# Attention with 16 queries against 2048 keys: another layout and place for the query load, two heads per matmul in P·V, and another order of work at the end

## The chip, the cores and the metric

The kernel runs on one core of one Trainium2 chip. The metric is device time in microseconds (us), taken as the median of several executions; lower is better. A core has a matrix engine (PE, with weight loads listed apart as PEld), a vector engine (DVE), a scalar engine (ACT), a general engine (POOL) and a sync engine (SP), which here issues all data transfers. Sixteen DMA engines move the data (the page gives the DMA shares as parts of 16). All executions quoted here are in the undisturbed ("fast") state.

## The reference

```python
B, H, Sq, Skv, Dh = 8, 16, 16, 2048, 256          # q, k, v in bf16
def reference(q, k, v):
    scale = q.shape[-1] ** -0.5
    scores = jnp.einsum('bhqd,bhkd->bhqk', q, k) * scale
    attn = softmax(scores, axis=-1)
    return jnp.einsum('bhqk,bhkd->bhqd', attn, v)
```

There are 128 heads (B·H). Each has only 16 queries, but its K and its V are 1 MB each. So 256 tiles of 1 MB are read, plus 1 MB of Q, and 1 MB of output is written.

## The kernel before

Four heads make a "quad"; there are 32 quads, numbered 0 to 31. For each head K is transposed on PE (16 f32 transposes, two bf16 values packed in each, into three buffers `stg` in PSUM, the memory in which this program puts PE's results; DVE and ACT copy them to `ktb`). For each quad come the scores (32 matmuls into `s_ps`, the four heads in four 32-column strips of the array), the max on DVE, the exp on ACT, the transposes of P (8), and P·V, called PV below (64 matmuls into `o_ps`). The order of work on PE is fixed in this list:

```python
NK = 4; NV = 8; NKT = 6; NSTG = 3       # K slots, V slots, transposed K, staging banks
# ... all Q transposes come first ...
for n in range(NQ):                      # NQ = 32 quads
    TK(4 * n)                            # transpose K of a head
    if n > 0: TP(n - 1)                  # transpose P of the quad before
    TK(4 * n + 1)
    if n > 0: pe_tasks.append(("PV", n - 1))
    TK(4 * n + 2)
    TK(4 * n + 3)
    pe_tasks.append(("S", n))            # scores
TP(NQ - 1)
pe_tasks.append(("PV", NQ - 1))
```

SP issues the loads in a fixed order too. A load waits until its slot is free, and then joins a queue of loads that are already on the way (five to eight of them for 246 of the 257 loads in the trace of the kernel before):

```python
sp.dma_start(qraw[:], qf).then_inc(sem_q, 16)     # Q first, in rows of 256 elements
# ... K and V alternate, V two heads behind K ...
for h in range(6, NH - 2):
    sp_loads.append(("K", h)); sp_loads.append(("V", h - VLAG))
sp_loads += [("K", NH - 2), ("K", NH - 1)] + [("V", h) for h in range(NH - 4, NH)]
```

And PV, one head per matmul, four heads side by side in four strips:

```python
for t in range(KT_T):                    # 16 pieces of 128 keys
    b, et = divmod(t, 2)
    for j in range(4):
        h = 4 * n + j
        c0 = (b * 128 + 32 * j) * 2
        lhs = ptb[:, n % 2, c0:c0 + 32].rearrange("p (q e) -> p q e", e=2)[:, :, et]
        last = pe.matmul(o_ps[32 * j:32 * j + 16, 0:DH], lhs,
                         vraw[:, h % NV, t * DH:(t + 1) * DH],
                         start=(t == 0), stop=(t == KT_T - 1), tile_position=(0, 32 * j))
last.then_inc(sem_pv, 1)
```

## Time and profile before

| | before |
|---|---|
| median | 666.59 us (664.53 to 668.14, 6 executions); 665.96 us over 16 executions in all |
| span of the profiled execution | 663.9 us |
| busy: PE, DVE, ACT | 71%, 41%, 39% |
| bytes moved, rate | 271.38 MB, about 421 GB/s in the middle |

The first fence is from the profile page of the kernel before: busy time of the engines, then the rows of 40 equal slices (DMA in tenths of busy, then GB/s), the queue that fetches instructions, and the shares of the chain that ended last. In such a chain "issue" is time in which an engine waited for nothing that the profile shows, and a q after an engine's name is its sequencer.

```profile
PE 472.1 (71%) x5392; PEld 371.1 (56%) x5392; DVE 271.4 (41%) x357; ACT 261.7 (39%) x386; POOL 0.8 (0%) x7
...
DMA  8999999999999999999999999999999999999991
GB/s 320 422 421 421 419 421 421 420 420 420 423 419 420 420 421 421 422 419 421 420 420 421 422 421 420 421 418 421 421 421 421 421 420 420 422 419 416 421 406 73
...
q8 instruction: 43, 0.70, 0.4%
...
DMA 69%; PE 24%; issue 3%; ACT 2%; DVE 1%; SPq 1%; ACTq 0%
```

The DMA row stays at 9 from the second slice to the last but one, at an even 420 GB/s or so. This was taken as the limit. The first slice (320 GB/s) and the last one (73 GB/s) are the only places where the stream is clearly not full, so the gain was looked for at these two ends.

The next fence holds PE's costliest groups, as listed by line (busy us, mean ns of one; then idle time before them), and after them a line from the view of the waits (us in total, times, longest).

```profile
L254 PE MATMUL stg<-ident,kraw 128*128 128x128 f32 x2048 | 291.8, 299 | 69.2 <-DMA kraw<-in_k_dram 66.7
L264 PE MATMUL stg<-ident,pbuf 128*128 128x128 f32 x256 | 47.9, 349 | 80.9 <-ACT pbuf L408 80.9
L291 PE MATMUL s_ps<-ktb,qtb 128*16 128x512 bf16 x1024 | 75.0, 440 | 24.2 <-DVE ktb L352 16.6
L320 PE MATMUL o_ps<-vraw,ptb 128*16 128x256 bf16 x2048 | 63.4, 277 | 6.2 <-DMA vraw<-in_v_dram 3.5
...
PE stg L254 <- DMA kraw<-in_k_dram: 66.7, 42, 3.9
```

PE is idle for 29% of the time, but only the 66.7 us in which it waits for K count as spare here: the other waits (80.9 us for the exp, for instance) are taken to be links of PE's own serial chain. Per quad the spare time is 66.7/32 = 2.1 us.

The chain at the very end, in order of time (start us, us, what), of the kernel before:

```profile
647.16 2.02 PE s_ps L291 x27
649.18 0.03 issue
649.21 2.30 DVE nmx L381
...
653.73 1.94 PE stg L264 x8
655.67 0.73 issue
656.41 3.55 PE o_ps L320 x64
...
660.18 0.48 DVE ostage L393
```

Scores, max, exp, transposes of P, PV and normalisation run one after another while the DMA engines have nothing left to do. The same stretch in the view by windows (window, its length, busy us of PE, PEld, DVE, ACT and POOL, then the granted PE clock (the share of full speed that the throttle allowed), the DMA share and GB/s):

```profile
650.00:655.00 5.00, 1.27 (x6) 1.30 (x7) 1.64 (x2) 2.06 (x2) 0.00 (x0) 0.79 0.26 105
655.00:660.00 5.00, 4.20 (x68) 2.64 (x66) 0.57 (x2) 0.60 (x1) 0.00 (x0) 0.53 0.01 3
```

The last PV ran at a granted clock of about a half and took 3.52 us; most of the others took 1.92.

The landing times of single loads are records in the trace. For the kernel before they show: Q landed at 7.36 us, K of head 0 at 9.85, the last K at 644.20, the last V at 654.06. The median distance between two landings of 1 MB is 2.486 us.

### The profile page before, as it was taken

Reading aid. Unit: us, or ns where it says so; the run is one execution under the profiler, and the core shown is the slowest. Engines: PE = TensorE matmul, PEld = TensorE weight load, DVE = VectorE, ACT = ScalarE, POOL = GpSimd, SP = SyncE. Lnnn points to the kernel's source line nnn. Section 1 sums busy time; section 2 is a strip of 40 time slices with the busy share of each in tenths; the row PEclk is TensorE's granted clock in tenths of the full one; section 3 lists DMA queues with packets and bytes.
Section 4 is the critical chain, followed back from the end, with each engine's and each line's share of the span. In section 5 each row is a group of like instructions: output and inputs, shape, how many; then the busy total and the mean of one; then the engine's idle time right before and its main releaser. Section 6 shows DMA issues by size and latency. Waiting matters only on the chain.

```text
span 663.9 us, 12939 instructions
## 1 busy us (share of the span) xinstructions
PE 472.1 (71%) x5392; PEld 371.1 (56%) x5392; DVE 271.4 (41%) x357; ACT 261.7 (39%) x386; POOL 0.8 (0%) x7
## 2 busy tenths in 40 slices
PE   5677667686877785866867767877776766668674
PEld 5455555565665574654656655655554655546562
DVE  4424443443344443343434433444343344434352
ACT  3414444333344334343434442444442344434341
POOL 0000000000000000000000000000000000000000
PEclk9879998988789889797998886888798899968887
DMA  8999999999999999999999999999999999999991
GB/s 320 422 421 421 419 421 421 420 420 420 423 419 420 420 421 421 422 419 421 420 420 421 422 421 420 421 418 421 421 421 421 421 420 420 422 419 416 421 406 73
DMA packets 41545, 271.38 MB, mean 409 GB/s; under 512 B 6160, under 2 KB 8208, under 8 KB 8720
## 3 DMA queue, kind: packets, MB, share of 16 engines
q1 hardware_dynamic: 41488, 270.56, 98.4%
q8 instruction: 43, 0.70, 0.4%
q14 instruction: 14, 0.11, 0.0%
HBM read 269.48 MB, written 1.05 MB: 407 GB/s over the span
## 4 chain that ended last, share of the span: by engine, by line
DMA 69%; PE 24%; issue 3%; ACT 2%; DVE 1%; SPq 1%; ACTq 0%
DMA kraw<-in_k_dram 69%; PE stg L254 17%; PE s_ps L291 3%; PE o_ps L320 2%; PE stg L264 2%; ACT pbuf L408 1%; DVE nmx L381 1%; SPq L198 0%; ACT ktb L354 0%; DVE ktb L352 0%; SPq L191 0%; DVE ostage L393 0%; SPq L203 0%; DVE rl L388 0%; ACTq L407 0%
## 5 line engine op out<-in xcount | busy, mean ns | idle before, releaser
L254 PE MATMUL stg<-ident,kraw 128*128 128x128 f32 x2048 | 291.8, 299 | 69.2 <-DMA kraw<-in_k_dram 66.7
L254 PEld LDWEIGHTS stg<-ident,kraw 128*128 128x128 f32 x2048 | 253.3, 154 | 114.2 <-issue 89.6
L354 ACT ACTIVATE ktb<-stg 128x512 f32<-128x512 f32 x287 | 175.4, 637 | 326.9 <-PE stg L254 326.9
L352 DVE COPY ktb<-stg 128x512 f32<-128x512 f32 x225 | 155.4, 691 | 139.0 <-PE stg L254 139.0
L381 DVE TENSOR_REDUCE nmx<-s_ps 128x1 f32<-128x2048 f32 x32 | 73.3, 2292 | 98.3 <-PE s_ps L291 98.3
L264 PE MATMUL stg<-ident,pbuf 128*128 128x128 f32 x256 | 47.9, 349 | 80.9 <-ACT pbuf L408 80.9
L291 PE MATMUL s_ps<-ktb,qtb 128*16 128x512 bf16 x1024 | 75.0, 440 | 24.2 <-DVE ktb L352 16.6
L264 PEld LDWEIGHTS stg<-ident,pbuf 128*128 128x128 f32 x256 | 38.5, 180 | 87.8 <-issue 87.8
L320 PE MATMUL o_ps<-vraw,ptb 128*16 128x256 bf16 x2048 | 63.4, 277 | 6.2 <-DMA vraw<-in_v_dram 3.5
L408 ACT ACTIVATE pbuf<-s_ps,nmx 128x2048 bf16<-128x2048 f32 x32 | 63.0, 1967 | 5.3 <-DVE nmx L381 4.5
L291 PEld LDWEIGHTS s_ps<-ktb,qtb 128*16 128x16 bf16 x1024 | 26.5, 95 | 62.3 <-DVE ktb L352 32.4
L320 PEld LDWEIGHTS o_ps<-vraw,ptb 128*16 128x16 bf16 x2048 | 50.3, 91 | 16.7 <-issue 10.8
L362 DVE COPY ptb<-stg 128x512 f32<-128x512 f32 x32 | 22.1, 692 | 81.4 <-PE stg L264 81.4
L364 ACT ACTIVATE ptb<-stg 128x512 f32<-128x512 f32 x32 | 19.1, 598 | 53.6 <-PE stg L264 53.6
L388 DVE RECIPROCAL rl<-lsum 128x1 f32<-128x1 f32 x32 | 5.2, 164 | 62.1 <-PE o_ps L320 62.1
L393 DVE TENSOR_SCALAR ostage<-o_ps,rl 128x256 bf16<-128x256 f32 x32 | 15.5, 484 | 1.1
L241 PE MATMUL stg<-ident,qraw 128*128 128x128 f32 x16 | 3.7, 424 | 7.4 <-DMA qraw<-in_q_dram 7.4
L241 PEld LDWEIGHTS stg<-ident,qraw 128*128 128x128 f32 x16 | 3.3, 226 | 7.4 <-DMA qraw<-in_q_dram 7.4
L408 ACT ACTIVATION_READ_ACCUMULATOR pbuf<-s_ps,nmx 128x1 f32 x32 | 6.3, 196 | 0.0
L342 ACT ACTIVATE qtb<-stg 128x1024 bf16<-128x1024 bf16 x2 | 2.0, 1025 | 8.0 <-PE stg L241 8.0
L340 DVE TENSOR_SCALAR qtb<-stg 128x1024 bf16<-128x1024 bf16 x2 | 1.4, 692 | 6.0 <-PE stg L241 6.0
L369 DVE MEMSET s_ps<- 128x2048 f32 x1 | 1.8, 1765 | 1.3 <-PEq L423 1.3
(9 smaller groups left out, 2.8 us busy)
## 6 DMA issues: line engine op xcount, KB each, us to landing
kraw<-in_k_dram SPq DMA_DIRECT2D x128, 1024.0 KB, 17.1
vraw<-in_v_dram SPq DMA_DIRECT2D x128, 1024.0 KB, 19.3
out_dram<-ostage SPq DMA_DIRECT2D x128, 8.0 KB, 14.2
qraw<-in_q_dram SPq DMA_DIRECT2D x1, 0.5 KB, 6.5
```

The lines of the kernel that those rows point to most:

```text
L241: last = pe.transpose(bank[:, i * 128:(i + 1) * 128], qraw32[:, tt, :], ident32[:])
L254: last = pe.transpose(bank[:, i * 128:(i + 1) * 128], kraw32[:, slot, kt * 128:(kt + 1) * 128], ident32[:])
L264: last = pe.transpose(bank[:, i * 128:(i + 1) * 128], pbuf32[:, n % 2, blk * 128:(blk + 1) * 128], ident32[:])
L291: last = pe.matmul(s_ps[32 * j:32 * j + 16, c * 512:(c + 1) * 512], lhs, rhs, start=(ed == 0), stop=(ed == 1), tile_position=(0, 32 * j),)
L320: last = pe.matmul(o_ps[32 * j:32 * j + 16, 0:DH], lhs, vraw[:, h % NV, t * DH:(t + 1) * DH], start=(t == 0), stop=(t == KT_T - 1), tile_p ...
L352: ins = eng.tensor_copy(dst, src)
L354: ins = eng.activation(dst, src, ACTF.Copy)
L362: ins = eng.tensor_copy(dst, src)
L364: ins = eng.activation(dst, src, ACTF.Copy)
L381: ve.tensor_reduce(nmx[:, b:b + 1], s_ps[:, :], axis=AX.X, op=ALU.max, negate=True).then_inc(sem_max, 1)
L393: ve.tensor_scalar(ostage[:, b, :], o_ps[:, 0:DH], rl[:, b:b + 1], None, op0=ALU.mult).then_inc(sem_norm, 1)
L408: ac.activation(pbuf[:, b, :], s_ps[:, :], ACTF.Exp, bias=nmx[:, b:b + 1], scale=1.0, accum_out=lsum[:, b:b + 1]).then_inc(sem_exp, 1)
```

## The change

The intent is threefold: make the query load cheaper and put it behind the first K; halve the number of PV matmuls by treating two heads in one; and let the stream of loads end with V alone, so that the long chain of the last quad (scores to exp) is finished before the last V lands.

```diff
-    qf = q.rearrange("b h s d -> (b h s) d").rearrange("(t p) d -> p t d", p=128)
+    qf = q.rearrange("b h s d -> (b h) (s d)")            # one row of 8 KB per head
...
     for n in range(NQ):
         TK(4 * n)
-        if n > 0:
+        if n == 0:
+            QF()                                          # Q transposes after the first K
+        if n > 0 and n < NQ - 1:
             TP(n - 1)
         TK(4 * n + 1)
-        if n > 0:
+        if n == NQ - 1:
+            TP(n - 1)
+        if n > 0 and not (TAIL and n == NQ - 1):
             pe_tasks.append(("PV", n - 1))
         TK(4 * n + 2)
         TK(4 * n + 3)
         pe_tasks.append(("S", n))
+    if TAIL:
+        pe_tasks.append(("PV", NQ - 2))                   # PV of quad 30 after the last scores
     TP(NQ - 1)
     pe_tasks.append(("PV", NQ - 1))
...
-        for h in range(6, NH - 2):
+        for h in range(6, NH - 4):
...
-        sp_loads += [("K", NH - 2), ("K", NH - 1)] + [("V", h) for h in range(NH - 4, NH)]
+        sp_loads += [("K", h) for h in range(NH - 4, NH)] + [("V", h) for h in range(NH - 6, NH)]
...
+    def pv_mode(n):
+        if n == NQ - 1:
+            return "last"
+        return "pair" if TAIL else "single"
...
+                    if mode == "pair":                    # two heads per matmul
+                        for t in range(KT_T):
+                            b, et = divmod(t, 2)
+                            for a in range(2):
+                                c0 = (b * 128 + 64 * a) * 2
+                                lhs = ptb[:, n % 2, c0:c0 + 128]...[:, :, et]
+                                last = pe.matmul(o_ps[64 * a:64 * a + 64, 0:2 * DH], lhs,
+                                    vraw[:, s0:s0 + 2, t * DH:(t + 1) * DH], ...,
+                                    tile_position=(0, 64 * a))
...
+                    else:                                 # "last": heads 0 to 2, then head 3
+                        for js in ((0, 1, 2), (3,)):
+                            for j in js: pe.wait_ge(...)   # V of these heads
+                            for t in range(KT_T):
+                                for j in js:
+                                    last = pv_single(t, j)
+                            last.then_inc(sem_pv, 1)
```

A pair matmul multiplies P of two heads with V of both. Half of each result (P of one head with V of the other) is never read. The normalisation is widened to 512 columns, the output takes the right half of each, and in the last quad the outputs of heads 0 to 2 are issued ahead of that of head 3.

## The prediction

> **What bounds the kernel now.** The DMA stream. The page shows the DMA engines at 9 tenths or more in 38 of 40 slices, at about 421 GB/s; the chain that ended last is 69% K loads. [...] The landing records show one 1 MB K or V tile every 2.486 us, the first at 9.8 us, the last at 654.1: 255 x 2.486 = 634 us plus 10 of excess, mostly six jumps of about 1.1 us, one per eight instruction fetches (43 of 16 KB). PE is busy 71%.
>
> **Outside the stream.** Head: the Q load comes first, in 2 KB packets, from 2.5 to 7.4 us; K0 lands 2.5 later. Tail: the last K lands at 644.2. Then the chain is transposes, scores (647.2), max 2.29, exp 2.16, transposes 1.94, PV 3.52 (1.92 elsewhere; granted clock 0.53 there), normalise, four output issues; the span ends at 663.9, 9.8 us after the last load.
>
> **What the change does.**
> 1. Q is read in 8 KB rows after K0: about 2.5 us of the stream, not 4.5. Estimate 1.3 to 2.3 us saved, on the path, as the whole stream moves earlier.
> 2. PV of two heads per matmul: 64 matmuls of 256 columns (four strips together) become 32 of 512 (two together): streamed time doubles, 1.92 to about 3.5 us a quad (estimate); normalise 0.48 to about 0.75. PE waits for K about 2.1 us a quad (66.7/32, view of the waits), so the added 1.6 should be absorbed, barely. PE instructions fall from 10784 to about 8800, fetches from 43 to about 35: one jump fewer, 1.1 us.
> 3. Tail order: the last K lands some 15 us before the end of the stream instead of 10. By the durations above, relative to that end: K127 transposed -11, scores -8.5, PV(30) -5, exp done -4, transposes -2, evictions -1, PV of heads 0 to 2 done +0.5 to +1.5, one strip alone for the last head 1.7 (3.4 at half clock), normalise 0.5, one output issue and landing 1.9. The end comes about 5 us after the last load instead of 9.8: 4 to 6 saved.
>
> Sum: 1.8 + 1.1 + 4.9, about 8 us. Steady state unchanged.
>
> **Predicted: 658.5 us, 80% range 655.0 to 662.5. Faster by over 2%: 0.05; within 2%: 0.93; slower by over 2%: 0.02.**
>
> **What would show the steps.** First K landing near 5.5 us, Q near 8. Median spacing still 2.486; about 35 fetches, five jumps. Pair PV: 992 matmuls, about 3.5 us a quad; PE's waits for K shrink from 66.7 us to 15 to 30, PE busy 77 to 80%. Last load near 651, span end about 5 us later. The DMA row stays at 9.
>
> **What would make it wrong.** If pair matmuls cost over 2 us extra a quad, PE becomes the bound, K slots free late, and gaps appear between loads: the gain vanishes. If PE in the tail (K every 2.5 us instead of 5, behind exp and max) runs late, the tail saving falls to 2 to 3. A halved clock in the last PV [...] costs 2 to 3. If the tail aligns perfectly, the end is 3.5 us after the last load, near 656.5.

That the rate has nothing left rests on the even 421 GB/s of the trace alone. The 3.5 us of a paired PV and the 1.7 us of a strip alone are estimates; in the trace of the kernel before, the matmuls of one strip start 0.108 us apart, and 16 times that is 1.73, twice that 3.46. The 2 to 3 us for a halved clock is an estimate too: the PV at 0.53 took 1.6 us longer than the others (3.52 against 1.92).

## The result, and the profile after

| | before | after |
|---|---|---|
| median | 665.96 us (16 executions) | 657.35 us (656.92 to 658.05, 7 executions) |
| ratio | | 0.9867, 95% interval 0.9854 to 0.9881 |
| span of the profiled execution | 663.9 us | 656.3 us |
| first two landings (K of head 0 and Q) both done | 9.85 us | 8.07 us |
| from there to the last landing (255 tiles) | 644.2 us | 643.9 us |
| from the last landing to the end | 9.8 us | 4.3 us |

A ratio is the mean time of one kernel's fast runs over that of the other's of the same rounds, so it is not quite the ratio of the medians. The change is 1.3% faster, which counts as "same" at a threshold of 2%, although it is clear of the noise.

The lower rows of the table split the span exactly: 1.8 us came from the head, 0.3 us (in this pair of traces) from the stream, 5.5 us from the tail. The page of the kernel after, the same lines:

```profile
PE 509.8 (78%) x4400; PEld 366.2 (56%) x4400; DVE 276.6 (42%) x358; ACT 260.3 (40%) x386; POOL 0.8 (0%) x7
...
DMA  8999999999999999999999999999999999999994
GB/s 364 420 420 422 418 421 422 420 419 419 422 420 419 422 421 421 421 421 418 421 423 417 422 421 420 423 421 419 420 422 420 421 422 420 420 422 421 417 403 204
...
q8 instruction: 35, 0.57, 0.4%
...
DMA 77%; PE 17%; issue 2%; DVE 1%; ACT 1%; SPq 1%; DVEq 0%; ACTq 0%
```

The middle of the stream is as it was. The first slice carries 364 instead of 320 GB/s, the last one 204 instead of 73: the stream starts fuller and the empty end is shorter. Eight blocks of instructions fewer are fetched.

PE's groups after, and its wait for K:

```profile
L274 PE MATMUL stg<-ident,kraw 128*128 128x128 f32 x2048 | 286.5, 294 | 40.1 <-DMA kraw<-in_k_dram 36.1
L358 PE MATMUL o_ps<-vraw,ptb 128*64 128x512 bf16 x992 | 116.6, 389 | 3.6 <-DMA vraw<-in_v_dram 2.9
L284 PE MATMUL stg<-ident,pbuf 128*128 128x128 f32 x256 | 40.9, 312 | 75.2 <-ACT pbuf L470 74.4
L311 PE MATMUL s_ps<-ktb,qtb 128*16 128x512 bf16 x1024 | 68.8, 411 | 24.2 <-DVE ktb L405 21.1
L341 PE MATMUL o_ps<-vraw,ptb 128*16 128x256 bf16 x64 | 3.8, 273 | 0.9 <-ACT ptb L417 0.7
...
PE stg L274 <- DMA kraw<-in_k_dram: 36.1, 40, 5.7
```

PV got dearer: 116.6 + 3.8 us instead of 63.4, or 3.65 us a quad instead of 1.92. The starts of the matmuls show how. Before, 64 matmuls of 256 columns went in 16 rounds of four, one in each strip, and the rounds started 0.108 us apart; after, 32 of 512 columns went in 16 rounds of two, 0.216 us apart. The number of rounds is the same, a round takes twice as long, and half of its results are thrown away. Yet PE's other groups got cheaper by 18.5 us together (K transposes 291.8 to 286.5, P transposes 47.9 to 40.9, scores 75.0 to 68.8), with the same instructions. The mean granted clock rose from 0.894 to 0.938. The other traces agree that the busier PE was granted more: 0.937 to 0.953 in the eight with pairing in all or nearly all quads (PE busy 76 to 78%), 0.889 to 0.912 in the six with pairing in one quad or none (71 to 72%). So the pairing paid for a third of its own cost, and 36.1 us of spare time are left.

The chain after, at its end (start us, us, what), and from the timeline the last transposes of P:

```profile
629.26 22.70 DMA vraw<-in_v_dram
651.96 0.04 issue
652.00 1.93 PE o_ps L341 x16
653.93 0.03 issue
653.95 0.49 DVE ostage L449
...
648.07 1.06 PE L284 MATMUL stg<-ident,pbuf 128*128 128x128 f32 x8 [1.00 <-ACT pbuf L470]
```

Before, the chain of the last quad ended the run. Now the landing of the last V does, followed by 16 matmuls, one normalisation and one output. The last transposes took 1.06 us instead of 1.94: the clock was full here (granted 1.00 from 645 to 655 us).

### The profile page after: what moved, and what is told of

The parts are those of the page before. It is cut to its first block, busy times and chain, and to the rows that moved or that the text cites. A ratio compares the mean times of both kernels' runs of the same rounds, so it can differ in the third digit from the quotient of the medians.

```text
span 656.3 us, 10925 instructions
## 1 busy us (share of the span) xinstructions
PE 509.8 (78%) x4400; PEld 366.2 (56%) x4400; DVE 276.6 (42%) x358; ACT 260.3 (40%) x386; POOL 0.8 (0%) x7
## 4 chain that ended last, share of the span: by engine, by line
DMA 77%; PE 17%; issue 2%; DVE 1%; ACT 1%; SPq 1%; DVEq 0%; ACTq 0%
DMA kraw<-in_k_dram 71%; PE stg L274 12%; DMA vraw<-in_v_dram 6%; PE o_ps L358 3%; PE s_ps L311 1%; DVE nmx L434 1%; PE stg L284 1%; DVE ktb L405 1%; SPq L217 0%; ACT pbuf L470 0%; PE o_ps L341 0%; PE stg L261 0%; ACT qtb L395 0%; DVE qtb L393 0%; SPq L210 0%
## 5 line engine op out<-in xcount | busy, mean ns | idle before, releaser
L274 PE MATMUL stg<-ident,kraw 128*128 128x128 f32 x2048 | 286.5, 294 | 40.1 <-DMA kraw<-in_k_dram 36.1
L274 PEld LDWEIGHTS stg<-ident,kraw 128*128 128x128 f32 x2048 | 244.0, 150 | 93.0 <-issue 59.8
L358 PE MATMUL o_ps<-vraw,ptb 128*64 128x512 bf16 x992 | 116.6, 389 | 3.6 <-DMA vraw<-in_v_dram 2.9
L284 PE MATMUL stg<-ident,pbuf 128*128 128x128 f32 x256 | 40.9, 312 | 75.2 <-ACT pbuf L470 74.4
L358 PEld LDWEIGHTS o_ps<-vraw,ptb 128*64 128x64 bf16 x992 | 59.4, 112 | 52.9 <-issue 12.4
L311 PE MATMUL s_ps<-ktb,qtb 128*16 128x512 bf16 x1024 | 68.8, 411 | 24.2 <-DVE ktb L405 21.1
L284 PEld LDWEIGHTS stg<-ident,pbuf 128*128 128x128 f32 x256 | 32.4, 158 | 82.1 <-issue 81.1
L455 DVE TENSOR_SCALAR ostage<-o_ps,rl 128x512 bf16<-128x512 f32 x31 | 23.3, 751 | 112.5 <-PE o_ps L358 112.5
L341 PE MATMUL o_ps<-vraw,ptb 128*16 128x256 bf16 x64 | 3.8, 273 | 0.9 <-ACT ptb L417 0.7
L341 PEld LDWEIGHTS o_ps<-vraw,ptb 128*16 128x16 bf16 x64 | 2.9, 89 | 1.8 <-DVE ptb L415 0.9
```

Of the source, the lines that this page charges most:

```text
L274: last = pe.transpose(bank[:, i * 128:(i + 1) * 128], kraw32[:, slot, kt * 128:(kt + 1) * 128], ident32[:])
L284: last = pe.transpose(bank[:, i * 128:(i + 1) * 128], pbuf32[:, n % 2, blk * 128:(blk + 1) * 128], ident32[:])
L311: last = pe.matmul(s_ps[32 * j:32 * j + 16, c * 512:(c + 1) * 512], lhs, rhs, start=(ed == 0), stop=(ed == 1), tile_position=(0, 32 * j),)
L341: return pe.matmul(o_ps[32 * j:32 * j + 16, 0:DH], lhs, vraw[:, h % NV, t * DH:(t + 1) * DH], start=(t == 0), stop=(t == KT_T - 1), tile_p ...
L358: last = pe.matmul(o_ps[64 * a:64 * a + 64, 0:2 * DH], lhs, vraw[:, s0:s0 + 2, t * DH:(t + 1) * DH], start=(t == 0), stop=(t == KT_T - 1), ...
L455: ve.tensor_scalar(ostage[:, b, 0:w], o_ps[:, 0:w], rl[:, b:b + 1], None, op0=ALU.mult).then_inc(sem_norm, 1)
```

## Experiments

Three questions: do the three parts add up; why does the pairing help although it doubles PE's work in PV; and which part of the tail counts. Kernels of one group (those with the same median in the column of the kernel before) ran on the same chip beside the kernel before. Only the group of e10 to e13 has the changed kernel in it (e10_again); the others are compared with it by their ratios and traces. The granted figures and landings below are those of the one execution whose trace was kept, the medians are of all.

| run | median us | before, same rounds | ratio (95%) | last landing to end, traced run | stream, 255 tiles | fetches |
|---|---|---|---|---|---|---|
| changed kernel | 657.35 | 665.96 | 0.9867 (0.9854 to 0.9881) | 4.3 | 643.9 | 35 |
| e1_single | 660.62 | 665.83 | 0.9917 (0.9887 to 0.9946) | 5.1 | 644.3 | 43 |
| e2_q_only | 663.69 | 665.83 | 0.9959 (0.9935 to 0.9984) | 9.5 | 644.4 | 43 |
| e3_tail_only | 661.75 | 665.83 | 0.9930 (0.9902 to 0.9958) | 4.7 | 644.8 | 43 |
| e4_pair_only | 665.47 | 665.83 | 0.9983 (0.9956 to 1.0010) | 12.0 | 642.8 | 35 |
| e10_again | 657.72 | 666.60 | 0.9863 (0.9841 to 0.9885) | 4.9 | 643.6 | 35 |
| e11_pair_30_only | 658.79 | 666.60 | 0.9883 (0.9861 to 0.9906) | 4.3 | 644.2 | 43 |
| e12_single_twice_30 | 659.04 | 666.60 | 0.9887 (0.9865 to 0.9908) | 4.8 | 644.7 | 44 |
| e13_pair_not_30 | 659.10 | 666.60 | 0.9885 (0.9863 to 0.9908) | 4.9 | 642.8 | 36 |
| e6_no_split | 660.27 | 665.51 | 0.9914 (0.9894 to 0.9934) | 7.6 | 643.0 | 35 |
| e7_old_loads | 660.06 | 665.51 | 0.9914 (0.9894 to 0.9934) | 7.2 | 643.0 | 35 |
| e5_q_rows_first | 657.75 | 665.51 | 0.9877 (0.9852 to 0.9902) | 4.3 | 643.4 | 35 |
| e14_halves | 657.35 | 665.51 | 0.9867 (0.9842 to 0.9892) | 4.5 | 643.2 | 35 |

The intervals are wide (about 0.25% either way) mostly because the kernel before scattered; the medians of one group may be compared more closely. All results were correct.

### The three parts alone

The query load alone (a cut, against the kernel before; the Q transposes also move behind the first K, the rest is as before):

```diff
-            sp.dma_start(qraw[:], qf).then_inc(sem_q, 16)        # 2 KB packets, ahead of K0
+                    if h == 0:                                   # after K0, rows of 8 KB
+                        sp.dma_start(qraw[:].rearrange("h s d -> h (s d)"), qf).then_inc(sem_q, 16)
```

> The kernel before with only the Q load changed (8 KB rows, after K0). Theory: the whole stream moves 1.8 us earlier and nothing else, so 664.2 us against 666.0, ratio 0.997; the distance from last load to the end stays 9.8 us. Rival (the head is hidden, the queue only waits longer later): no change.

Measured: 663.69 us against 665.83, ratio 0.9959. K of head 0 landed at 5.74 us and Q at 8.18, against 9.85 for both before (1.7 us earlier), and the distance from the last landing to the end was 9.5 us, as good as unchanged. The head start was handed through to the end: the 255 tiles took 644.4 us, against 644.2 before.

The tail alone (load order, PE order, split of the last PV; old Q load, no pairing; a cut, against the changed kernel):

```diff
-        return "pair" if TAIL else "single"
+        return "single"                                          # and the old Q load
```

> The kernel before with only the tail changed (last four K ahead of six V, PV of the last but one quad after the last scores, last quad's PV split). Theory: distance from the last load to the end falls from 9.8 to 4.3 us, stream unchanged: about 660.5 us, ratio 0.992. Rival (tail is shared with the pairing): less than 4 us.

Measured: 661.75 us, ratio 0.9930; from the last landing to the end 4.7 us instead of 9.8. About 4.1 to 4.7 us, a little less than expected; the traced stream was 0.6 us longer, and why was not looked into.

The pairing alone (old Q load, old tail, last quad one head per matmul; the mode in short):

```diff
+        return "single" if n == NQ - 1 else "pair"               # old loads, old PE order
```

> The kernel before with only the pairing, in all quads but the last. Theory: fetches fall to 35, which shortens the stream by 0.3 us as in the changed kernel, and PV of the last but one quad, 1.7 us longer, now lies on the old tail chain ahead of the last transposes: 0 to 1.5 us slower than before, about 667. Rival (fewer instructions pay): 1.1 us or more faster. Rival (pairing alone makes PE the bound): 670 or more.

Measured: 665.47 us, ratio 0.9983 with 1 inside the interval: no clear change. The trace, of the slowest of the six executions (666.38 us), shows the two halves of the expectation working against each other. The stream was 1.4 us shorter than before (0.3 was expected); the tail was 2.1 us longer (12.0 instead of 9.8), since PV of quad 30 now takes 3.65 us and stands ahead of the last K transposes. Chain at the end of this run:

```profile
640.43 3.59 PE o_ps L350 x32
...
645.55 2.05 PE stg L266 x16
...
655.40 1.94 PE stg L276 x8
```

The three ratios multiply to 0.9959 · 0.9930 · 0.9983 = 0.987, which is the ratio of the whole change (0.9867). The parts add up within their intervals. Without the pairing they fit less well: query load and tail alone give 0.9959 · 0.9930 = 0.989, and the kernel with just these two (e1_single, next) measured 0.9917, with an interval that begins at 0.9887.

### What the pairing does within the whole change

First it was taken away:

```diff
-        return "pair" if TAIL else "single"
+        return "single"
```

> The changed kernel with PV back to one head per matmul (64 of 256 columns, four strips together) in every quad; new Q load and new tail kept. Theory (the DMA stream bounds both, pairing only spends PE slack and spares some instruction fetches): fetches back to 43, stream from first to last tile within 0.5 us of the changed kernel, median about 657.6 us, so equal to the changed kernel within 0.5 us. Rival 1 (the pairing carries the gain): back to 662 us or more. Rival 2 (the pairing costs, since it doubles PE time in PV): faster than the changed kernel by 1 us or more, near 656. PE's waits for K grow from 36 us to about 60 to 67 us.

Measured: 660.62 us (659.16 to 663.33), about 3 us slower than the changed kernel and with a range of 4.2 us instead of 1.1. The theory expected at most 0.5 us, so it missed. PE's wait for K was 81.7 us (60 to 67 were expected), well above the 36.1 of the changed kernel: PE had more spare time and the run was slower all the same. The fetches alone do not explain 3 us either. The trace of this run shows something else in the tail (timeline: start us, us, what, and what ended the wait; then a window with the granted clock as the third figure from the right):

```profile
647.10 1.94 PE L284 MATMUL stg<-ident,pbuf 128*128 128x128 f32 x8 [2.50 <-ACT pbuf L470]
...
650.16 5.01 PE L341 MATMUL o_ps<-vraw,ptb 128*16 128x256 bf16 x64 [1.12 <-DMA vraw<-in_v_dram]
...
647.10:653.90 6.80, 5.67 (x62) 4.26 (x63) 0.77 (x3) 0.60 (x1) 0.00 (x0) 0.50 0.30 121
```

For 6.8 us, just in the last transposes and the last PV, the clock was halved. PV of quad 30 is shorter without pairing, so PE stood idle for 2.5 us under the max and the exp of the last quad. New theory: pairing acts in two ways, by fewer fetches (a shorter stream) and by filling that gap (a full clock at the end). Four kernels on one chip were to tell these apart.

> The changed kernel as it is, once more, so that the three next to it have it on the same chip. Both theories: 657.4 us within 0.5, granted clock about 0.94.

Measured: 657.72 us (656.95 to 658.54). It agrees with the first measurement of the changed kernel. Its trace, however, has 3.4 us at half clock in the last PV, and its end came 4.9 us after the last landing instead of 4.3:

```profile
646.54 1.06 PE L284 MATMUL stg<-ident,pbuf 128*128 128x128 f32 x8 [0.78 <-ACT pbuf L470]
...
649.54 4.71 PE L341 MATMUL o_ps<-vraw,ptb 128*16 128x256 bf16 x64 [1.93 <-DMA vraw<-in_v_dram]
```

So the pairing does not always keep the clock full.

Pairing in quad 30 alone:

```diff
+        return "pair" if n == NQ - 2 else "single"
```

> The changed kernel with pairing in quad 30 alone (the last but one), one head per matmul in all the others. Taking the pairing away everywhere cost 3.3 us, which the fetches alone do not explain. Clock theory (the longer paired PV of quad 30 fills PE's gap under the max and exp of the last quad, so that the clock is not halved in the last transposes and the last PV): the tail is as short as in the changed kernel (4.3 us from last load to end, last transposes near 1.1 us), only the fetches are back at 43: 658.4 us, at most 1.2 us slower. Fetch theory (the stream gets shorter by fewer fetches, and that is all): as without pairing, 660.6 us.

Measured: 658.79 us, 1.1 us slower than the changed kernel beside it (658.30 to 659.31 against 656.95 to 658.54, so the ranges overlap a little); the clock theory allowed 1.2, the fetch theory asked for 3. Its tail:

```profile
648.47 1.06 PE L284 MATMUL stg<-ident,pbuf 128*128 128x128 f32 x8 [1.00 <-ACT pbuf L470]
...
650.27 3.97 PE L341 MATMUL o_ps<-vraw,ptb 128*16 128x256 bf16 x64 [0.73 <-ACT ptb L417]
...
649.40:652.80 3.40, 2.53 (x55) 1.97 (x54) 0.97 (x3) 0.60 (x1) 0.00 (x0) 1.00 0.26 98
```

With one paired quad of 31 the clock was full in the last stretch and the end came 4.3 us after the last landing, as in the first trace of the changed kernel.

No pairing, but PV of quad 30 done twice:

```diff
+                        for r in range(2 if n == NQ - 2 else 1):
                             for t in range(KT_T):
                                 for j in range(4):
                                     last = pv_single(t, j)
```

> The changed kernel without any pairing, but with the PV of quad 30 done twice over (the second pass starts the sums anew, so the result is right): 1.9 us of pure waste on PE. Clock theory: the waste keeps PE busy before the last quad, so the tail is as short as in the changed kernel, 658.4 us, faster than the 660.6 us without the waste. Fetch theory: 660.6 us or more.

Measured: 659.04 us (658.53 to 659.41). With this pure waste on PE the kernel without pairing measured faster: its ratio is 0.9887 against 0.9917, its median 1.6 us lower, and the scatter is gone. The two ran in different groups and the intervals overlap, so this alone is support, not proof; and in the traced execution the clock was halved all the same, for 3.4 us, in the last PV (the last transposes were at full clock, 1.07 us), and the end came 4.8 us after the last landing, not the 4.3 expected.

Pairing everywhere but in quad 30:

```diff
+        return "single" if n == NQ - 2 else "pair"
```

> The changed kernel with pairing in every quad but 30 and the last. Clock theory: fetches stay near 35 and the stream stays as short as in the changed kernel, but the last transposes (1.9 us) and the last PV run at half clock: 1.5 to 2.5 us slower than the changed kernel, 659 to 660. Fetch theory: 657.4 us, the same as the changed kernel.

Measured: 659.10 us (657.51 to 660.17), 1.4 us slower than the changed kernel beside it, just under what the clock theory expected (1.5 to 2.5), where the fetch theory expected nothing. With five executions each, the ranges overlap (657.51 to 660.17 against 656.95 to 658.54), so this too is support only. The execution whose trace was kept is the fastest of the five:

```profile
645.85 1.07 PE L284 MATMUL stg<-ident,pbuf 128*128 128x128 f32 x8 [2.74 <-ACT pbuf L470]
...
648.61 4.63 PE L341 MATMUL o_ps<-vraw,ptb 128*16 128x256 bf16 x64 [1.69 <-DMA vraw<-in_v_dram]
```

There the last transposes ran at full clock (1.07 us), against the expectation, and only the last PV at half, just as in the trace of e10_again. Its span, 655.8 us, is below those of the changed kernel's two traces (656.3 and 656.8). The slower ones have no trace, so where they lose is not shown.

The fetch half of the theory can be read from all the traces. In the eight kept traces with 35 or 36 fetches the 255 tiles took 642.8 to 643.9 us, mean 643.2; in the six with 43 or 44 they took 644.2 to 644.8, mean 644.4. The two sets do not overlap: 1.2 us for eight fetches of 16 KB. The fetch count goes together with the pairing in these kernels, so the sets alone do not name the cause. The landing times point to the fetches: of the 83 distances above 3 us between two landings (the median is 2.486) in the 14 traces, every one ends 2.1 to 4.2 us after the start of a fetch, and 74 after the 1st, 9th, 17th, 25th, 33rd or 41st. In the trace of the kernel before there are six, one after each of these, and they exceed the median by 0.9 to 1.4 us, 6.9 us together; with 35 or 36 fetches there is no 41st. This one pair of traces does not show the gain by itself, though: the changed kernel's trace has seven such distances (four after the 1st, 9th, 17th and 25th fetch, three after the 18th, 26th and 34th), which exceed the median by 0.7 to 1.3 us, 7.1 us together, and its stream is only 0.3 us shorter. A fetch in the traces moves 16384 bytes and takes about 1.07 us on a DMA engine. Eight of them are 131 KB, which at 421 GB/s would take 0.3 us, less than the 1.2 us between the two sets.

### Which part of the tail counts

The old order of the last loads, all else as changed:

```diff
-        for h in range(6, NH - 4):
+        for h in range(6, NH - 2):
...
-        sp_loads += [("K", h) for h in range(NH - 4, NH)] + [("V", h) for h in range(NH - 6, NH)]
+        sp_loads += [("K", NH - 2), ("K", NH - 1)] + [("V", h) for h in range(NH - 4, NH)]
```

> The changed kernel with the old order of the last loads (the last two K ahead of four V). Theory: the last K lands 5 us later, so the chain of scores, max, exp and transposes ends after the last load instead of before it: the end comes 7.6 us after the last load instead of 4.3, 660.7 us, up to 662.5 where the clock is halved. Rival (splitting and reordering PE's work are what matters): within 1 us of the changed kernel.

Measured: 660.06 us; from the last landing to the end 7.2 us. The chain of this run again hangs on the last K:

```profile
625.84 15.38 DMA kraw<-in_k_dram
...
652.54 3.25 PE o_ps L341 x64
```

The load order is worth 2.9 us of the 5.5 (7.2 against 4.3).

The last PV in one piece:

```diff
         if n == NQ - 1:
-            return "last"
+            return "single"
```

> The changed kernel with the last quad's PV in one piece (64 matmuls after the last V has landed) instead of three heads ahead and one after. Theory: PE needs as long for 64 matmuls four strips wide (1.92 us) as for 16 in one strip (1.91 us), so PE loses nothing, but all four output issues now follow the last normalisation: 1.3 us slower, 658.7. If PE's clock halves while it waits for the last V: 2.9 us slower, 660.3. Rival (the split is what makes the tail short): 4 us slower or more.

Measured: 660.27 us; from the last landing to the end 7.6 us, the case with the halved clock. PE waited 4.4 us for the last V, and then:

```profile
651.07 3.59 PE L341 MATMUL o_ps<-vraw,ptb 128*16 128x256 bf16 x64 [4.37 <-DMA vraw<-in_v_dram]
```

At full clock these 64 matmuls take 1.92 us (most PVs of the kernel before), as long as the 16 of one strip in the split version (1.91, trace of the changed kernel; one starts 0.11 us after the other, as the rounds of four do). So the split saves no matmul time as such. It saves 1.3 us of output issues (three of them, each some 0.45 us after the one before: in the trace of the kernel before the four start at 660.69, 661.05, 661.51 and 661.97 us), and here the 1.7 us of the halved clock, since PE is at work while the last V is on its way. Load order and split are each worth about 3 us, and they are not independent: both serve to have only a small remainder after the last landing. The third part of the new tail, PV of quad 30 after the last scores, was not undone alone, so its share is not known.

Q ahead of K of head 0, but in rows of 8 KB:

```diff
+            sp.dma_start(qraw[:].rearrange("h s d -> h (s d)"), qf).then_inc(sem_q, 16)
             for kind, h in sp_loads:
...
-                    if h == 0:
-                        sp.dma_start(qraw[:].rearrange("h s d -> h (s d)"), qf).then_inc(sem_q, 16)
```

> The changed kernel with Q again ahead of K0, still in 8 KB rows. Theory (Q's gain is the shorter time in the stream, 2.5 us instead of about 4.3, and its place does not matter): 657.4 us, within 0.5 of the changed kernel. Rival (its gain is that K0 lands first and PE starts earlier): 1 to 2 us slower.

Measured: 657.75 us, the same as the changed kernel (0.9877 against 0.9867, intervals overlapping). Both loads had landed at 8.12 us, against 8.07 in the changed kernel, although PE's first transpose came 2.5 us later (8.25 instead of 5.71 us). The rows of 8 KB made the gain: with Q first in both, the two loads had landed at 8.12 us here and at 9.85 in the kernel before, whose page counts 512 packets of 2 KB to under 8 KB where that of this kernel counts none. The place of Q made none.

### An attempt to do better

After the last landing 16 matmuls of one strip are left. The last two V were loaded in halves, first halves first:

```diff
+        sp_loads += [("Va", NH - 2), ("Va", NH - 1), ("Vb", NH - 2), ("Vb", NH - 1)]
...
+                        for t in range(KT_T // 2):               # first halves, all four heads
+                            for j in range(4):
+                                pv_single(t, j)
+                        for i, js in enumerate(((0, 1, 2), (3,))):
+                            pe.wait_ge(sem_vb[i], 16)            # second half of head 2, then of head 3
+                            for t in range(KT_T // 2, KT_T): ...
```

> An attempt to do better: the last two V are loaded in halves, first halves of both ahead of the second halves, and the last PV takes the first halves of all four heads before it waits. After the last landing 8 matmuls of one strip are left instead of 16: 0.95 us faster than the changed kernel, 656.4 us. If rows of 4 KB slow the stream, or the PE chain is not ready in time, no gain.

Measured: 657.35 us (656.41 to 657.68). No gain that the intervals could show, beside an expected 0.95 us. In the trace 8 matmuls were left after the last landing, as planned, but they took 1.9 us instead of 0.95: PE had been ready early, had waited 2.4 us for the first halves, and its clock was halved from 649.8 to 653.2 us.

```profile
649.06 4.29 PE L350 MATMUL o_ps<-vraw,ptb 128*16 128x256 bf16 x64 [2.37 <-DMA vraw<-in_v_dram]
```

In this trace the saving in work was eaten by the clock. Whether some filler work in that gap would bring the 0.95 us was not tried.

## Why the prediction was right

It forecast 658.5 us (655.0 to 662.5); 657.35 was measured. Point by point:

- **What bounds the kernel.** Right. The rate in the middle, 421 GB/s, is the same in both kernels, and a head start of 1.7 us (the query load alone) reached the end almost in full.
- **Step 1, the query load: 1.3 to 2.3 us.** Right: 1.8 us in the trace. First K at 5.58 us and Q at 8.07, forecast 5.5 and 8. The text left open whether size or place does it; it is the size.
- **Step 2, the pairing.** PE time right: 3.65 us a quad (forecast about 3.5), 992 matmuls, PE busy 78% (77 to 80). The fetches fell to 35, as forecast, and the stream was shorter by 1.2 us in the mean of all traces (forecast 1.1), though by only 0.3 in the first pair of traces. Two things were missed. The wait for K fell to 36.1 us only, not to 15 to 30; the busier PE got a better clock and did its other work 18.5 us faster. And the forecast counted the longer PV(30) as merely harmless in the tail, whereas it seems to help the clock there: without it in that one quad the median was 1.4 us longer, though with overlapping ranges.
- **Step 3, the tail: 4 to 6 us.** Right: 5.5 us in the trace (end 4.3 us after the last load, forecast about 5). The list of times held within about a microsecond, the last item within 1.7: relative to the last landing the last K was transposed at -11.2 us (forecast -11), scores ended at -8.5 (-8.5), PV(30) at -4.9 (-5), evictions at -2.2 (-1), and heads 0 to 2 were done at about -0.2 (+0.5 to +1.5).
- **The sum.** About 8 us forecast, 7.6 in the pair of traces, 8.6 between the medians. In that pair some luck helped: a stream gain 0.8 us below the forecast and a tail gain 0.6 us above it nearly cancel. With the mean stream gain of 1.2 us the three parts make 8.5.

How firmly the causes stand: that the load order and the split of the last PV shorten the tail is shown by undoing each (7.2 and 7.6 us after the last landing instead of 4.3), and that the rows of 8 KB make the head, not the place of Q, by undoing the place (8.12 us against 8.07). That the stream is 1.2 us shorter with eight fetches fewer is what fourteen traces show in the mean; that the fetches are the cause is inferred from where the delays fall (74 of 83 after the 1st, 9th, 17th, 25th, 33rd or 41st).

That the pairing in quad 30 helps by the clock is supported, not shown. The medians of one kernel with it alone, one with waste work in its place and one with it alone removed all lie on the side that the clock theory expected, but each within reach of the scatter. In the traces with the new tail the clock stayed full to the end in three of the four with that pairing and the last PV split as in the changed kernel (ends 4.3 us after the last landing, and 4.9 in the fourth, e10_again), and in none of the four without it (4.7 to 5.1 us; e12 with its waste work is one of them, so filler work did not keep the clock full there). The two traces of the changed kernel itself differ: full to the end in one, 3.4 us at half in the other. The last section shows what goes with it: the clock changes in steps of 3.41 us, which lie differently in the traces of the kernel before and of the changed kernel. Alone the pairing had no clear effect (0.9983); taking it out of the whole change cost more (0.9917 against 0.9867, or 3.3 us between the medians). Of these 3.3 us, 1.2 are the stream and 0.8 the longer tail of the one trace of the unpaired kernel. About 1.3 us remain open. That kernel scattered over 4.2 us and was not measured a second time, so part of them may be its own scatter.

## What to carry to other kernels

Where one stream of loads bounds the kernel from end to end, look at its two ends (here worth 1.8 and 5.5 us): how soon the first large load runs at full rate, and how much serial work is left after the last byte lands; order the last loads so that those with the longest chain behind them come first, and cut the final step so that only a small remainder waits for the last load. Count as spare time what an engine waits for the bounding stream (here 66.7 us; PE took on 37.7 us of busy time, this wait fell to 36.1, and the stream did not get longer), not all of its idle time. Work that fills such a gap may even pay if it keeps the matrix engine's clock up (supported here, not shown). In a kernel bound by DMA, count instruction fetches too: with eight fewer the stream was 1.2 us shorter in the mean here.

## What the traces show of fetches and of the clock

- Instruction fetches and the data stream: with 35 or 36 fetches instead of 43 or 44 (about 1.07 us each on a DMA engine), 255 loads of 1 MB took 1.2 us less in the mean (643.2 against 644.4 us), and of the 83 landings over 3 us after the one before, 74 came after the 1st fetch or an eighth one from there (in the traces of the kernel before and of the changed kernel such a landing was late by 0.7 to 1.4 us).
- The clock and PE's idle gaps: in one execution of the changed kernel the longest gap in the tail was 1.93 us, with 1.06 us of transposes before it, and the clock was halved in the next 3.4 us. The two windows of that run (e10_again; granted clock third from the right):

```profile
645.80:649.20 3.40, 1.06 (x8) 0.85 (x8) 1.51 (x3) 1.20 (x3) 0.00 (x0) 1.00 0.55 220
649.20:652.60 3.40, 3.06 (x48) 2.27 (x52) 0.00 (x0) 0.00 (x0) 0.00 (x0) 0.50 0.10 41
```

PV of quad 30 had ended at 645.77 us, just before the first of these windows began, and so did not count in it. The clock records come in steps: in the traces of the kernel before and of the changed kernel every complete record lasts a multiple of 3.413 us, at 1.0 or at 0.5 (the half-clock stretches are 3.4, 6.8 and 10.2 us long). Counted from the start of the span, the edges lie at 0.95 us and at 0.25 us plus multiples of that step, so they lie differently in the two executions.

The 14 traces together (their clock records cut into windows of 3.4 us, from 20 us on) show what goes before a halved window. Of 2171 windows at full clock, 337 were followed by one at half clock: PE was busy for at most 1.71 us in each of these, and for at least 1.36 us in each of the other 1834. The longest gap tells the two kinds apart less well (1.2 to 3.4 us against up to 2.05 us). So in these traces the PE work within a whole window tells them apart better than the longest gap alone; a rule for other kernels it is not. The scatter of the unpaired kernel (659.16 to 663.33 us) would fit steps that lie differently in each execution, but its slower executions have no trace.
